# MLP first layer as a 2x2 block product with seven block products, its weight factors kept in DRAM

## The chip, the cores and the metric

The kernel runs on one core of one Trainium2 chip. The time is in device microseconds (us) for one execution. The engines are TensorE (PE in the profile, with PEld for its weight loads), VectorE (DVE), ScalarE (ACT), GpSimd (POOL) and SyncE (SP), which issues the transfers (DMA). All arithmetic is in float32.

## The reference

An attention block with normalised queries and keys feeds a two-layer MLP.

```python
batch, n_heads, seq, head_dim = (8, 12, 448, 64)
q_n, k_n = (rmsnorm(q, g_q), rmsnorm(k, g_k))
attn = softmax(q_n @ k_n.T / sqrt(head_dim))        # per batch and head
x = (attn @ v), heads side by side                  # 3584 tokens x 768
h = x @ w_in                                        # 768 x 2048
out = (h - tanh(h)) @ w_out                         # 2048 x 768
```

The weights arrive as float64, and the kernel rounds them to float32 itself.

## The kernel before

**Two streams on one TensorE.** The work is in 8 batches of 448 tokens. Attention goes by steps `s`, 48 of them: batch `b` and a pair of heads `hp`, six steps (`NP`) for each batch. A step normalises (`norm`, `norm_q`), transposes (`turn`), makes the scores and their exponentials in two halves (`scores`), multiplies with v (`values`), sums the exponentials (`totals`), and divides (`divide`: a reciprocal of 448 columns and a product on VectorE), which leaves one tile `xT` of 128 features x 448 tokens. The MLP of batch `b` runs beside the attention of batch `b+1`: `slot(s)` writes the attention step and, at four places in it, calls `run(gap)`, which takes matmuls from the stream `mlp()` until `gap` ns of it are written. The stream is `hidden(b)`, the first layer, and then `project(b)`, the second. The first six attention steps have no MLP beside them (`first_slot`), and the MLP of batch 7 has no attention beside it (`run(1e9)` at the end).

**The order is the program's.** The instructions stand on each engine as the Python code writes them (a manual schedule); each engine works through its own list and waits on semaphores, SP's list of transfers included.

**First layer.** `hidden(b)` makes, for each of 16 blocks `f` of 128 hidden features, six matmuls (`c`, blocks of 128 input features) of 128 x 128 weights by 448 columns into one bank of PSUM; then ScalarE makes tanh and VectorE subtracts it (`gT`). A float32 matmul stands in the trace as two weight loads and two passes. The weights `w_in_sb` lie in SBUF for the whole run.

**Second layer.** `project(b)` makes for each of three (four in odd batches) blocks of 128 tokens and each half `n` of 384 output columns 16 matmuls of 384 columns. `EARLY`, `weight(to)` and `weight_load(n)` are the weights' way in: 64 pieces of 384 KB in float64 words (32 of `w_in`, 32 of `w_out`) are loaded and rounded by `round_weight_a` (ScalarE, two instructions, L71 and L72), `round_weight_b` (VectorE, three: L78, L79, L82) and `round_weight_c` (GpSimd, L90). Twenty pieces are done by the end of the first six steps, 28 more inside `hidden(0)`, 16 inside `project(0)`.

## Time and profile before

| | |
|---|---|
| time, median of 3 runs | 1652.33 us (1651.37 to 1653.82) |
| the profiled execution's own time | 1652.88 us |
| its span, first to last instruction | 1651.0 us |
| PE busy | 1595.7 us, 97% |
| PE matmuls of line L338 (first layer) | 1536 passes, 598.9 us |
| PE matmuls of line L378 (second layer) | 1536 and 256 passes, 516.6 and 85.4 us |
| DVE, ACT, POOL busy | 633.1, 402.6, 320.5 us |
| bytes moved by DMA | 70.22 MB, mean 43 GB/s |

A row of the timeline has the start, the time taken and the engine, line, operation and tiles of one instruction or of several alike (xN). A row of the windows has a stretch, its length, and the busy time of each engine in it with the number of instructions. In the table of groups the two numbers behind the bar are the busy time of all and the mean ns of one. A row of the waits has the total, how often, and the longest.

### The profile page before, as it was taken

Reading aid. Unit: us, or ns where it says so; the run is one execution under the profiler, and the core shown is the slowest. Engines: PE = TensorE matmul, PEld = TensorE weight load, DVE = VectorE, ACT = ScalarE, POOL = GpSimd, SP = SyncE. Lnnn points to the kernel's source line nnn. Section 1 sums busy time; section 2 is a strip of 40 time slices with the busy share of each in tenths; the row PEclk is TensorE's granted clock in tenths of the full one; section 3 lists DMA queues with packets and bytes.
Section 4 is the critical chain, followed back from the end, with each engine's and each line's share of the span. In section 5 each row is a group of like instructions: output and inputs, shape, how many; then the busy total and the mean of one; then the engine's idle time right before and its main releaser. Section 6 shows DMA issues by size and latency. Waiting matters only on the chain.

```text
span 1651.0 us, 14103 instructions
## 1 busy us (share of the span) xinstructions
PE 1595.7 (97%) x5512; PEld 793.5 (48%) x5512; DVE 633.1 (38%) x769; ACT 402.6 (24%) x765; POOL 320.5 (19%) x222
## 2 busy tenths in 40 slices
PE   3889998999999999999999999999999999999998
PEld 1334454544554445544455444554455544555554
DVE  5788877234323432243333334323432243221100
ACT  4454453222221222122212221112222122201100
POOL 4644444111111112111211112111211111000000
PEclk8999999999999999999999999999999999999999
DMA  9432243100111011001001100110001100000000
GB/s 244 120 104 75 67 141 110 45 17 17 29 46 32 17 25 35 31 22 33 23 27 34 41 17 17 32 48 17 17 27 48 31 17 23 11 15 5 1 19 21
DMA packets 93585, 70.22 MB, mean 43 GB/s; under 512 B 48453, under 2 KB 89413, under 8 KB 93509
## 3 DMA queue, kind: packets, MB, share of 16 engines
q1 hardware_dynamic: 93184, 69.23, 14.8%
q8 instruction: 45, 0.74, 0.2%
q14 instruction: 32, 0.25, 0.0%
q10 hardware_dynamic: 324, 0.00, 0.0%
HBM read 58.20 MB, written 11.01 MB: 42 GB/s over the span
## 4 chain that ended last, share of the span: by engine, by line
PE 91%; DVE 4%; DMA 2%; issue 1%; POOL 1%; ACT 1%; SPq 0%; ACTq 0%; POOLq 0%; DVEq 0%
PE mm L338 35%; PE mm L378 33%; PE sc L271 9%; PE av L298 9%; PE dn L310 3%; DMA w_raw<-in_moe_w_out_dram 1%; PE sc L249 1%; PE sc L254 1%; DMA k_nat<-in_k_dram 1%; DVE rd L319 1%; POOL sq L224 1%; DVE rr L225 0%; DVE w_in L79 0%; DVE w_out L79 0%; DVE w_in L82 0%
## 5 line engine op out<-in xcount | busy, mean ns | idle before, releaser
L338 PE MATMUL mm<-xT,w_in 128*128 128x448 f32 x1536 | 598.9, 544 | 3.2 <-DVE gT L345 1.7
L378 PE MATMUL mm<-w_out,gT 128*128 128x384 f32 x1536 | 516.6, 492 | 3.7 <-POOL w_out L90 3.7
L338 PEld LDWEIGHTS mm<-xT,w_in 128*128 128x128 f32 x1536 | 284.9, 190 | 300.3 <-issue 283.2
L378 PEld LDWEIGHTS mm<-w_out,gT 128*128 128x128 f32 x1536 | 286.9, 191 | 228.0 <-issue 36.0
L276 ACT ACTIVATE p<-sc,rr 112x448 f32<-112x448 f32 x384 | 211.9, 637 | 405.4 <-PE sc L271 322.8
L319 DVE RECIPROCAL rd<-dn 128x448 f32<-128x448 f32 x48 | 141.9, 2956 | 202.0 <-PE dn L310 201.6
L345 DVE TENSOR_TENSOR gT<-mm,th 128x448 f32<-128x448 f32 x128 | 79.7, 623 | 333.6 <-ACT th L344 333.6
L344 ACT ACTIVATE th<-mm 128x448 f32<-128x448 f32 x128 | 69.6, 544 | 465.6 <-PE mm L338 458.6
L271 PE MATMUL sc<-qT,kT 64*112 64x448 f32 x768 | 173.7, 567 | 3.2 <-ACT qT L258 3.2
L224 POOL TENSOR_TENSOR sq<-k_nat 112x512 f32<-112x512 f32 x48 | 51.5, 1073 | 629.2 <-DMA k_nat<-in_k_dram 629.2
L298 PE MATMUL av<-p,v_nat 112*64 112x448 f32 x768 | 156.4, 549 | 6.8 <-issue 6.8
L228 POOL TENSOR_TENSOR rr<-rr,neg_half 112x16 f32<-112x16 f32 x48 | 139.3, 2902 | 51.0 <-DVE rr L227 47.8
L290 DVE TENSOR_TENSOR sum<-sum,p 112x896 f32<-112x896 f32 x84 | 94.3, 1123 | 93.3 <-ACT p L276 88.0
L271 PEld LDWEIGHTS sc<-qT,kT 64*112 64x112 f32 x768 | 63.2, 174 | 101.0 <-issue 86.4
L225 DVE TENSOR_REDUCE rr<-sq 112x8 f32<-112x512 f32 x96 | 65.6, 683 | 109.8 <-POOL sq L224 109.8
L298 PEld LDWEIGHTS av<-p,v_nat 112*64 112x64 f32 x768 | 52.3, 138 | 100.3 <-issue 100.3
L224 POOL TENSOR_TENSOR sq<-q_nat 112x512 f32<-112x512 f32 x48 | 49.9, 1039 | 240.7 <-DVE rr L225 240.7
L378 PE MATMUL mm<-w_out,g_rest 128*128 128x384 f32 x256 | 85.4, 489 | 0.0
L235 DVE TENSOR_TENSOR n<-q_nat,rr 112x512 f32<-112x512 f32 x48 | 42.0, 875 | 95.0 <-PE sc L254 72.8
L388 DVE COPY o_sb<-mm 128x384 f32<-128x384 f32 x28 | 15.5, 555 | 158.2 <-PE mm L378 157.9
L378 PEld LDWEIGHTS mm<-w_out,g_rest 128*128 128x128 f32 x256 | 47.9, 190 | 35.6 <-issue 4.1
L386 ACT COPY o_sb<-mm 128x384 f32<-128x384 f32 x28 | 13.4, 478 | 189.3 <-PE mm L378 125.1
(49 smaller groups left out, 598.6 us busy)
## 6 DMA issues: line engine op xcount, KB each, us to landing
w_out<-in_moe_w_in_dram SPq DMA_DIRECT2D x32, 384.0 KB, 7.6
k_nat<-in_k_dram SPq DMA_DIRECT2D x96, 112.0 KB, 3.1
q_nat<-in_q_dram SPq DMA_DIRECT2D x48, 224.0 KB, 3.5
v_nat<-in_v_dram SPq DMA_DIRECT2D x48, 224.0 KB, 3.4
w_raw<-in_moe_w_out_dram SPq DMA_DIRECT2D x24, 384.0 KB, 3.1
out_dram<-o_sb SPq DMA_DIRECT2D x48, 192.0 KB, 1.9
w_out<-in_moe_w_out_dram SPq DMA_DIRECT2D x8, 384.0 KB, 3.3
out_dram<-o_sb SPq DMA_DIRECT2D x16, 96.0 KB, 2.2
```

The costliest lines, as they stand in the source:

```text
L224: nc.gpsimd.tensor_tensor(out=sq, in0=rows, in1=rows, op=ALU.mult)
L225: nc.vector.reduce_sum(rr[:, i], sq, axis=AX.X)
L228: nc.gpsimd.tensor_tensor(out=rr2, in0=rr2, in1=neg_half, op=ALU.pow)
L271: nc.tensor.matmul(sc[:CP, :S], lhsT=kT[r, c * CP : (c + 1) * CP], rhs=qT[r, :], start=True, stop=True)
L276: nc.scalar.activation(p[:, h, i, :], tiles[h][:CP, :S], AF.Exp, scale=rr[:, 0, 2 * c + h : 2 * c + h + 1])
L290: nc.vector.tensor_tensor(out=t, in0=t, in1=part, op=ALU.add)
L298: nc.tensor.matmul(av[h * D : (h + 1) * D, :S], lhsT=v_nat[:, h, c, :], rhs=p[:, h, c % 2, :], start=(c == 0), stop=(c == NCH - 1),)
L319: nc.vector.reciprocal(rd, dn[:, :S])
L338: nc.tensor.matmul(hps[:, :S], lhsT=w_in_sb[f][:, c, :], rhs=xT[b, c], start=(c == 0), stop=(c == CD - 1))
L344: nc.scalar.activation(th, hps[:, :S], AF.Tanh, bias=0.0, scale=1.0)
L345: nc.vector.tensor_tensor(out=g[:, f, :], in0=hps[:, :S], in1=th, op=ALU.subtract)
L378: nc.tensor.matmul(ops[:, :HALF], lhsT=lhs[:, f, :], rhs=w_out_sb[f][:, d], start=(f == 0), stop=(f == CF - 1),)
```

## The change

Each batch's product of 448 tokens x 768 by 768 x 2048 is taken as 2 x 2 blocks (tokens in halves of 224, input features in halves of 384, hidden features in halves of 1024) and made with seven block products in place of eight (a scheme of the Strassen kind with shared sums). `hidden(b)` works in four sets `j` (two blocks of 128 from each half of the hidden features), each of seven products in the order `ORDER`; a product is six matmuls of 128 x 128 weights by 224 columns into one bank, and adds up in PSUM with another one where the scheme lets it (`first` false). Sums between banks are made on VectorE and GpSimd, copies out of a bank on ScalarE.

The seven weight factors of each set are made once (`combine_weights`, eight rounded pieces to seven factors), written to DRAM (`keep_weights`, seven stores of 384 KB), and read back for each product of each batch into a ring of eight tiles (`ring_load`), seven products ahead. `w_in_sb` is gone. The factors of the tokens' side are made in `divide` from the pair of `xT` tiles three steps apart (VectorE for batch 0, GpSimd after). Raw pieces are prefetched up to 6 ahead (14 before). In `first_slot` and `slot` the sums of the exponentials and the reciprocal now come ahead of the product with v. The four gaps of a slot are sized by batch; for batch 0 the whole first layer goes into two slots and the second layer into four. The core of the diff:

```diff
+    HS = S // 2
+    HC = CD // 2
+    SETS = CF // 4
+    ORDER = (1, 6, 5, 2, 7, 3, 4)
...
+    ring = pool("ring", bufs=8)
+    scratch = pool("scratch", bufs=1, space=bass.MemoryType.DRAM)
...
-    ps_v = pool("ps_v", bufs=1, space=PSUM)
-    ps_m = pool("ps_m", bufs=2, space=PSUM)
+    ps_m = pool("ps_m", bufs=1, space=PSUM)
+
+    def mm_bank(tag):
+        return ps_m.tile([P, 512], F32, name=tag, bufs=2 if tag == "mb" else 1)
...
-    w_in_sb = [weights.tile([P, CD, P], F32, name=f"w_in{f}") for f in range(CF)]
+    w_in_dram = {
+        (j, p): scratch.tile([P, 2 * HALF], F32, name=f"w_in{j}_{p}") for j in range(SETS) for p in range(1, 8)
+    }
...
+    stage = gp.tile([P, CF, S], F32, name="gT").bitcast(I32).rearrange("p f s -> p (f s)")
+    NSTAGE = CF * S // DM
...
+    def built(j, p):
+
+        return w_out_sb[CF // 2 * (j % 2) + p].rearrange("p (f n) -> p f n", f=2)
...
         if n < 2 * CF:
+            j, f, blk = n // 8, n % 8 // 4, n % 4
+            p, low, i = ((1, 0, 0), (0, 1, 0), (4, 1, 1), (2, 0, 1))[blk]
+            return 2 * j + f + low * CF // 2, i, built(j, p)[:, f]
...
+        if n < EARLY:
+            raw = stage[:, n % NSTAGE * DM : (n % NSTAGE + 1) * DM].rearrange("p (f w) -> p f w", w=2)
...
-        if n < CF or 0 <= n - 2 * CF - CF // 2 < 3:
-            return True
-        return n - (CF if n < 2 * CF else CF // 2 if n < 2 * CF + CF // 2 else 3) < done[2]
+        if n < EARLY:
+            return n - NSTAGE < done[2]
+        return n - 4 < max(done[2], EARLY)
...
+            finish_weights(n - 1 if n < EARLY else n)
+            while done[0] < min(n + 6, 4 * CF) and place_free(done[0]):
                 weight_load(done[0])
                 done[0] += 1
+            if kept[1] < kept[0] and n >= 8 * kept[0] + 3:
+                keep_weights()
...
+            if done[2] % 8 == 0 and done[2] <= 2 * CF:
+                combine_weights(done[2] // 8 - 1)
+
+    def combine_weights(j):
+        a = [built(j, p) for p in range(8)]
+        nc.vector.tensor_tensor(out=a[5], in0=a[0], in1=a[4], op=ALU.add)
+        nc.gpsimd.tensor_tensor(out=a[7], in0=a[1], in1=a[0], op=ALU.subtract)
+        nc.vector.tensor_tensor(out=a[6], in0=a[5], in1=a[1], op=ALU.subtract)
+        nc.vector.tensor_tensor(out=a[3], in0=a[2], in1=a[6], op=ALU.subtract)
+        kept[0] = j + 1
+
+    def keep_weights():
+        j = kept[1]
+        for p in ORDER:
+            nc.sync.dma_start(out=w_in_dram[j, p], in_=built(j, p).rearrange("p f n -> p (f n)"))
+        kept[1] = j + 1
...
+    ring_steps = [(b, j, p) for b in range(B) for j in range(SETS) for p in ORDER]
+    ring_tiles = {}
+
+    def ring_load(to):
+
+        for n in range(len(ring_tiles), min(to, len(ring_steps))):
+            b, j, p = ring_steps[n]
+            assert kept[1] > j
+            t = ring_tiles[ring_steps[n]] = ring.tile([P, 2, HC, P], F32, name="w_f")
+            nc.sync.dma_start(out=t.rearrange("p f c n -> p (f c n)"), in_=w_in_dram[j, p])
...
-    def totals(s):
-        dn = ps_v.tile([P, 512], F32, name="dn")
...
-        return dn
-
-    def divide(s, av, dn):
-        b, hp = steps[s]
         rd = sp.tile([P, S], F32, name="rd")
         nc.vector.reciprocal(rd, dn[:, :S])
+        return rd
+
+    def divide(s, av, rd):
+        b, hp = steps[s]
         x = xT[b, hp] = xp.tile([P, S], F32, name="xT")
...
+        if hp < HC:
+            return
+        c = hp - HC
...
+        eng = nc.vector if b == 0 else nc.gpsimd
+        x11, x12, x21, x22 = (xT[b, r][:, n : n + HS] for r in (c, hp) for n in (0, HS))
+        t1, t2, t4 = (tt[b][:, i, c] for i in range(3))
+        eng.tensor_tensor(out=t1, in0=x12, in1=x11, op=ALU.subtract)
+        eng.tensor_tensor(out=t2, in0=x22, in1=t1, op=ALU.subtract)
+        eng.tensor_tensor(out=x12, in0=x22, in1=x12, op=ALU.subtract)
+        eng.tensor_tensor(out=t4, in0=x21, in1=t2, op=ALU.subtract)
...
+        def product(j, p, bank, first):
             if b == 0:
-                weight(EARLY + (3 * CF - EARLY) * (f + 1) // CF)
-            for c in range(CD):
-                nc.tensor.matmul(
-                    hps[:, :S], lhsT=w_in_sb[f][:, c, :], rhs=xT[b, c], start=(c == 0), stop=(c == CD - 1)
-                )
+                weight(EARLY + k + 1)
+            ring_load(k + 7)
+            w = ring_tiles[b, j, p]
+            ring_tiles[b, j, p] = None
+            for f in range(2):
+                for c in range(HC):
+                    nc.tensor.matmul(
+                        bank[:, f * HS : (f + 1) * HS], lhsT=w[:, f, c, :], rhs=moving[p](c),
+                        start=(first and f == 0 and c == 0), stop=(f == 1 and c == HC - 1),
+                        skip_group_check=not first,
+                    )
+                    if f == 0 or c < HC - 1:
+                        yield 4 * HS / ENGINE_NS
+            now = later[:]
+            later.clear()
+            for fn in now:
+                fn()
...
+        pending = None
+        for j in range(SETS):
+            ma = mm_bank("ma")
+            yield from product(j, 1, ma, True)
+            s1 = part("s1", 2)
+            nc.scalar.copy(out=s1, in_=view(ma))
+            yield took
+            if pending:
+                yield from pending()
+            mb = mm_bank("mb")
+            yield from product(j, 6, mb, True)
+            s2 = part("s2", 2)
+            nc.vector.tensor_tensor(out=s2, in0=view(mb), in1=s1, op=ALU.add)
+            yield took
+            mc = mm_bank("mc")
+            yield from product(j, 5, mc, True)
+            s5 = part("s5")
+            nc.scalar.copy(out=s5, in_=view(mc))
+            yield took
+            yield from product(j, 2, ma, False)
+            shrink(j, 0, low, view(ma), nc.vector)
+            yield took
+            yield from product(j, 7, mb, False)
+            u3 = part("u3")
+            nc.vector.tensor_tensor(out=u3, in0=view(mb), in1=s1, op=ALU.add)
+            nc.gpsimd.tensor_tensor(out=u3, in0=u3, in1=s5, op=ALU.add)
+            later.append(lambda j=j, u3=u3: shrink(j, 1, high, u3, nc.gpsimd))
+            yield took
+            yield from product(j, 3, mc, False)
+            nc.vector.tensor_tensor(out=s2, in0=view(mc), in1=s2, op=ALU.add)
+            later.append(lambda j=j, s2=s2: shrink(j, 0, high, s2, nc.gpsimd))
+            yield took
+
+            def pending(j=j, mb=mb, s1=s1):
+                yield from product(j, 4, mb, False)
+                nc.vector.tensor_tensor(out=s1, in0=view(mb), in1=s1, op=ALU.add)
+                later.append(lambda: shrink(j, 1, low, s1, nc.gpsimd))
+                yield took
+
+        yield from pending()
+        for fn in later:
+            fn()
...
+        ring_load(SETS * 7 * (b + 1) + 7)
...
-    per_slot = (4 * S / ENGINE_NS * CF * CD + 4 * HALF / ENGINE_NS * CF * 7) / NP
+    H_NS = 4 * HS / ENGINE_NS * 7 * 6 * SETS
+    O_NS = 4 * HALF / ENGINE_NS * 2 * CF
+
+    def gap_ns(s):
+
+        b = s // NP - 1
+        if b == 0:
+            return H_NS / 8 if s % NP < 2 else O_NS * FULL / (4 * (NP - 2))
+        return (H_NS + O_NS * (FULL + b % 2)) / (4 * NP)
...
-            av = values(s)
+            rd = totals(s, mm_bank("mc"))
...
+            av = values(s, mm_bank("ma"))
...
-        divide(s, values(s), totals(s))
+        rd = totals(s, sc_bank())
+        divide(s, values(s, sc_bank()), rd)
```

On TensorE, at the start of `hidden(1)`, before, from the last rows of `project(0)` on (`mm` the MLP's bank, `sc` the scores' bank; a row's last number counts matmuls, each of them two passes):

```order
L378 MATMUL mm<-w_out_164,gT 128x384
L338 MATMUL mm<-xT,w_in_133 128x448 x6
L249 MATMUL sc<-ident,k_nat 128x112 x4
L254 MATMUL sc<-ident,n 128x112 x4
L338 MATMUL mm<-xT,w_in_134 128x448 x6
L338 MATMUL mm<-xT,w_in_135 128x448 x2
L271 MATMUL sc<-qT,kT 112x448 x4
```

The same place after (`w_f` a tile of the ring, `tt` a sum of blocks of `xT`, `ma`, `mb`, `mc` the MLP's banks; L353 is `values`, L365 `totals`, now ahead of it):

```order
L427 MATMUL ma<-xT,w_f 128x224 x6
L427 MATMUL mb<-tt,w_f 128x224 x6
L427 MATMUL mc<-tt,w_f 128x224 x5
L365 MATMUL sc<-sum,ones 64x448 x2
L353 MATMUL sc<-p,v_nat 64x448 x8
L427 MATMUL mc<-tt,w_f 128x224
L427 MATMUL ma<-xT,w_f 128x224 x6
```

The six matmuls of 448 columns for one weight block have become six of 224 columns for one product, each product with weights from the ring, and a bank is asked for again two or more products later.

On SP, in the second slot of `hidden(0)`, before: raw pieces of the second layer's weights between the loads of q, k and v.

```order
L180 DMA w_out_157<-in_moe_w_out_dram 128x768
L144 DMA k_nat<-in_k_dram 112x4x64 x2
L147 DMA q_nat<-in_q_dram 112x2x256
L180 DMA w_out_158<-in_moe_w_out_dram 128x768
L180 DMA w_out_159<-in_moe_w_out_dram 128x768
```

The same place after (L206 a raw piece, L257 a store of `keep_weights`, L269 a load of the ring):

```order
L206 DMA w_raw_1375<-in_moe_w_out_dram 128x768
L257 DMA w_in3_1_175<-w_out9_147 128x768
L257 DMA w_in3_6_180<-w_out14_152 128x768
L257 DMA w_in3_5_179<-w_out13_151 128x768
L257 DMA w_in3_2_176<-w_out10_148 128x768
L257 DMA w_in3_7_181<-w_out15_153 128x768
L257 DMA w_in3_3_177<-w_out11_149 128x768
L257 DMA w_in3_4_178<-w_out12_150 128x768
L269 DMA w_f_1384<-w_in3_1_175 128x768
L206 DMA w_raw_1404<-in_moe_w_out_dram 128x768
L269 DMA w_f_1406<-w_in3_6_180 128x768
```

Seven stores now stand in the list ahead of the load that reads the first of them back, and every raw piece has a ring load beside it.

On VectorE, in the first slot of `hidden(0)`, after (L78, L79, L82 round one piece; L248, L250, L251 are `combine_weights`; L467 and L472 add banks). Before, such a stretch holds only pieces and L345 (`gT`), one L345 for about two pieces.

```order
L78 TENSOR_SCALAR w_out_140<-w_out_140 128x384
L79 TENSOR_SCALAR w_out_140<-w_out_140 128x384
L82 SCALAR_TENSOR_TENSOR w_out_140<-w_raw,w_out_140 128x384
L248 TENSOR_TENSOR w_out_143<-w_out_138,w_out_142 128x768
L250 TENSOR_TENSOR w_out_144<-w_out_143,w_out_139 128x768
L251 TENSOR_TENSOR w_out_141<-w_out_140,w_out_144 128x768
L467 TENSOR_TENSOR u_1104<-mb,s_1000 128x448
L78 TENSOR_SCALAR w_out_147<-w_out_147 128x384
L79 TENSOR_SCALAR w_out_147<-w_out_147 128x384
L82 SCALAR_TENSOR_TENSOR w_out_147<-w_raw,w_out_147 128x384
L472 TENSOR_TENSOR s_1019<-mc,s_1019 128x448
```

The additions that free a bank for TensorE now stand behind the three instructions of a piece and, once in seven products, behind the three of `combine_weights`.

82 lines of the change are left out of this document (44 added, 38 removed).

## The prediction

> **What bounds the kernel now.** I read the page first: the busy shares and the chain that ended last.
>
> ```profile
> PE 1595.7 (97%) x5512; PEld 793.5 (48%) x5512; DVE 633.1 (38%) x769; ACT 402.6 (24%) x765; POOL 320.5 (19%) x222
> PE 91%; DVE 4%; DMA 2%; issue 1%; POOL 1%; ACT 1%; SPq 0%; ACTq 0%; POOLq 0%; DVEq 0%
> ```
>
> TensorE carries the span, so only its work and its waits count. Next come the windows, cut where the first six steps' start-up ends (46), where the MLP of batch 0 begins (118.5), where its first layer ends (217), where batch 1's MLP begins (316.24), and one later batch.
>
> ```profile
> 0.00:46.00 46.00, 13.76 (x48) 6.68 (x49) 26.04 (x42) 18.33 (x36) 25.30 (x23) 0.85 0.89 231
> 46.00:118.50 72.50, 65.66 (x329) 26.64 (x328) 54.40 (x68) 38.95 (x78) 41.76 (x29) 0.98 0.44 120
> 118.50:217.00 98.50, 95.28 (x313) 44.55 (x313) 86.55 (x127) 47.27 (x97) 43.64 (x36) 1.00 0.24 71
> 217.00:316.24 99.24, 92.19 (x321) 46.64 (x320) 59.82 (x86) 34.18 (x68) 38.41 (x30) 0.97 0.34 102
> 316.24:511.00 194.76, 194.76 (x677) 96.78 (x675) 66.19 (x74) 41.21 (x77) 30.90 (x19) 1.00 0.10 29
> ```
>
> The columns after the length are PE, PEld, DVE, ACT, POOL, clock, DMA share, GB/s. From 316 on TensorE never stops, and every other engine is under 35% busy. While weights are rounded (118.5 to 217) VectorE is at 88%. So there are two regimes: seven batches bound by TensorE alone, and batch 0, where the weights' way in is nearly as long as the matmuls.
>
> The price of a pass is cleanest at the end, where the MLP of batch 7 runs alone (timeline of TensorE).
>
> ```profile
> 1490.12 72.32 PE L338 MATMUL mm<-xT,w_in 128*128 128x448 f32 x192
> 1562.28 62.08 PE L378 MATMUL mm<-w_out,gT 128*128 128x384 f32 x192
> 1624.20 20.80 PE L378 MATMUL mm<-w_out,g_rest 128*128 128x384 f32 x64
> ```
>
> From start to start: 72.16 us for 192 passes of 448 columns, 375.8 ns each; 61.92 us for 192 of 384, 322.5 ns. That is 0.833 ns a column and 2.5 ns fixed.
>
> **The change, term by term.**
>
> *First layer, the gain.* Before, 96 matmuls a batch, 192 passes of 448. After, 28 products of six matmuls, 336 passes of 224. By the line above a pass of 224 takes 189.1 ns, 63.5 us a batch in place of 72.2: 8.6 us less.
>
> No row shows a float32 pass that short with 128 rows and 128 columns of weights, so I bound it. These rows show small passes and the weight loads (PEld):
>
> ```profile
> 320.75 0.55 PE L249 MATMUL sc<-ident,k_nat 112*128 112x112 f32 x4
> 321.13 0.55 PE L254 MATMUL sc<-ident,n 112*128 112x112 f32 x4
> 321.52 6.19 PE L338 MATMUL mm<-xT,w_in 128*128 128x448 f32 x16
> 353.47 0.55 PE L249 MATMUL sc<-ident,k_nat 112*128 112x112 f32 x4
> 354.15 0.30 PEld L338 LDWEIGHTS mm<-xT,w_in 128*128 128x128 f32 x2
> 1490.49 0.19 PEld L338 LDWEIGHTS mm<-xT,w_in 128*128 128x128 f32 x1 [0.19 <-issue]
> 1490.87 0.19 PEld L338 LDWEIGHTS mm<-xT,w_in 128*128 128x128 f32 x1 [0.19 <-issue]
> ```
>
> Four transposes of 112 columns, each with its own load, take 0.38 us from start to start, 96 ns each: on the same line, so a load behind each short pass cost nothing there. A load of the first layer takes 190 ns by itself, but two of them end within 0.30 us, so a second one begins about 110 ns after the first. Loads start with the pass before (1490.49 is one pass after 1490.12) and are over half-way through it. If only the 110 ns must fit beside a pass of 187 ns, it does. If the whole 190 ns must, a pass takes 190 to 192, and the gain falls by 0.3 to 1.0 us a batch. The good end is the proportional one, 187.9 ns: 0.4 us more. I take 189.1, the fit of two rows of the same form. Not hidden at all is a rival below.
>
> The Trainium skill speaks against this: its page "TensorE: Matmul & The Clock Gate", Part 3, under "The mechanism", says that a weight load overlaps matmuls in flight only when it goes to another row group. All loads here take all 128 rows, so by that rule they would overlap nothing. The trace disagrees at 448 columns, where 375.8 ns a pass leaves no room for a load.
>
> *What goes with it in batches 1 to 7.* For each set ScalarE has six instructions in place of four (544 ns by the group below), VectorE five in place of four (623), GpSimd four new ones of 448 columns (about 940 by its 512 columns in 1073). GpSimd also gets twelve of 224 columns a batch, about 0.5 us each.
>
> ```profile
> L345 DVE TENSOR_TENSOR gT<-mm,th 128x448 f32<-128x448 f32 x128 | 79.7, 623 | 333.6 <-ACT th L344 333.6
> L344 ACT ACTIVATE th<-mm 128x448 f32<-128x448 f32 x128 | 69.6, 544 | 465.6 <-PE mm L338 458.6
> L224 POOL TENSOR_TENSOR sq<-k_nat 112x512 f32<-112x512 f32 x48 | 51.5, 1073 | 629.2 <-DMA k_nat<-in_k_dram 629.2
> ```
>
> That is 4.4 us more on ScalarE, 2.5 on VectorE and 21 on GpSimd for a batch of some 186 us, where they had 41, 66 and 31. All stay under 70 us, and a bank is asked for again at least two products (4.5 us) later, so TensorE covers it; without that cover each late sum would show in full. I allow 0.5 us a batch for short waits at the products' seams, 0 to 2 for the range.
>
> The ring brings 28 x 384 KB = 11.0 MB a batch. The rows that price a transfer:
>
> ```profile
> q1 hardware_dynamic: 93184, 69.23, 14.8%
> w_raw<-in_moe_w_out_dram SPq DMA_DIRECT2D x24, 384.0 KB, 3.1
> 15.00:25.00 10.00, 4.83 (x16) 2.14 (x16) 8.15 (x13) 5.99 (x13) 7.05 (x6) 1.00 1.10 332
> ```
>
> 69.23 MB in 14.8% of 1651 us is 283 GB/s while it moves; the fullest stretch had 332. So 11.0 MB take 33 to 39 us of a first layer that lasts about 90 us beside attention and 63.5 alone, asked for seven products ahead (16 us, against 3.1 to land). Hidden. On SP each ring load waits for the product eight before it; the q, k and v loads queued behind stand in program order near the same matmuls and have two slots of lead.
>
> *Batch 0.* Between the two transposes at 320.75 and 353.47 lies one slot, with four runs of 16 passes: 32.72 - 64 x 0.3758 = 8.7 us of attention on TensorE a slot. Before, batch 0 took 197.7 us (118.5 to 316.24) for 72.2 + 61.9 + 6 x 8.7 = 186.3 us of matmuls; the other 11 are waits:
>
> ```profile
> PE mm L378 <- POOL w_out L90: 3.7, 2, 2.7
> PE sc L271 <- ACT qT L258: 2.6, 1, 2.6
> PE mm L338 <- DVE gT L345: 1.7, 1, 1.7
> PE mm L338 <- DVE xT L321: 1.5, 1, 1.5
> PE av L298 <- issue: 6.8, 5, 1.4
> ```
>
> (the last is of the first six steps). After, the first layer and its 28 pieces share two slots, 63.5 + 2 x 8.7 = 81 us on TensorE. VectorE in these slots, by the groups of the window 118.5 to 217:
>
> ```profile
> L79 DVE TENSOR_SCALAR w_in<-w_in 128x384 int32<-128x384 int32 x14 | 9.3, 665 | 0.5
> L82 DVE SCALAR_TENSOR_TENSOR w_in<-w_out,w_in 128x384 int32<-128x384 int32 x14 | 9.3, 661 | 0.5
> L78 DVE TENSOR_SCALAR w_in<-w_in 128x384 f32<-128x384 f32 x14 | 6.1, 433 | 0.0
> L288 DVE TENSOR_TENSOR sum<-p 112x896 f32<-112x896 f32 x3 | 3.8, 1271 | 0.0
> ```
>
> A piece is 1.76 us, 28 are 49. Twenty additions at 623 are 12.5. Six of `combine_weights`, 768 columns against 896 in 1271, are 6.5. Attention has (66.19 - 16 x 0.623 - about 2 for outputs) / 6 = 9 us a slot, 18. Together 86 us, now more than TensorE, and before VectorE lost 12 of 98.5 us to waits of its own. The transfers in the same stretch: 28 raw pieces, 28 ring loads, 14 stores (sets 2 and 3) and up to 7 of set 1, 77 x 0.393 MB, and 1.4 MB of q, k, v: 31.7 MB, 95 us at 332 GB/s and 112 at 283, of which the last 10 us of the first steps take a part. So 87 (VectorE alone, no waits) to 112; I take 100, since two resources at their limit seldom fit together. The second layer's four slots are 61.9 + 4 x 8.7 = 96.7 plus 6 for waits (16 pieces in two of them; 10 before with 44 pieces in six slots): 102.7. Batch 0 becomes 202.7, 5.0 more.
>
> The skill's page "DMA: Bandwidth & Descriptors", in its table at the top, has about 358 GB/s as the limit of HBM for a core. By that figure those bytes would take an estimated 89 us, and the term would be some 5 us less.
>
> *The first 118.5 us.* The chain there:
>
> ```profile
> 11.55 12.88 SPq L175 DMA_DIRECT2D w_out<-in_moe_w_in_dram x12
> 24.60 0.93 SPq L144
> 25.58 8.51 DMA k_nat<-in_k_dram
> 34.24 1.05 POOL sq L224
> ```
>
> and on GpSimd:
>
> ```profile
> 24.56 3.42 POOL L90 TENSOR_TENSOR w_in<-w_in,w_out 128x384 int32<-128x384 int32 x3
> ```
>
> SP issued 12 raw pieces before the third step's k, which landed at 34.1. With six pieces ahead rather than 14 it issues four there, so k lands some 10 us earlier; GpSimd is free for it from 28, so 6 us come off. The 6.8 us of "av <- issue" go too if VectorE lets them: `totals` now stands first, so its reciprocal runs beside scores and `values`. But VectorE gets six combining additions (6.5 us) and twelve small ones (about 4): 54.4 + 10.5 = 65 of 72.5 us, so I count 2 of the 6.8. What is late next is the first ring tile: seven stores of set 1 (2.75 MB, 8.3 to 9.7 us) are queued ahead of it, about one step before the first product; 4 us. Net -4, between -12 and +6.
>
> **The sum**, against the profiled execution, 1652.88 us, which is its span of 1651.0 and 1.9 around it, and 0.5 above the median:
>
> - batches 1 to 7: -7 x 8.6 = -60.3
> - seams: +3.5
> - batch 0: +5.0
> - start: -4
>
> 1652.9 - 55.8 = 1597.
>
> **Rivals.**
>
> 1. *Batch 0 becomes a chain through DRAM.* The factors of a set can be read only after pieces, combination and stores; the ring cannot run ahead of that. If nothing covers it, each of sets 1 to 3 costs 9.7 us of stores and 3.1 to land, 38 in all, on top of the sum in place of my 4 at the start: about 1631. For it: VectorE at 88% already and the seven stores ahead of the first load. Against: eight products lie between combining a set and needing it.
> 2. *The ring is late in every batch.* If SP's waits let only one load at a time be under way, a product alone lasts 3.1 us and not 2.27; 21 products of batch 7 then cost 17 us more, and beside attention (a product each 3.1 us or so) nothing unless q, k and v loads collide, some 3 us a batch: 1614 to 1635. Against: eight buffers.
> 3. *Slower: weight loads are not hidden behind short passes.* Place: every first-layer pass. If a pass takes 187 + 110 = 297 ns, a batch costs 99.8 us, 27.6 more than before, eight times 221: about 1870. It decides from 72.16 / 336 = 215 ns a pass on. For it: the load's 190 ns is as long as the pass, and PEld would be near 100% in the first layer. Against: the transposes at 96 ns. It is what the skill's rule on row groups would do here.
>
> **Chances and range.** My forecast 0.70, rival 1 0.12, rival 2 0.06, rival 3 0.06; 0.03 for a start and batch 0 that both gain (around 1578), 0.03 for mishaps that eat the gain within 0.2% or beyond. A change under 0.2% (3 us) is about what a measurement of this kernel can't tell from none. Faster: 0.70 + 0.12 + 0.06 + 0.03, less 0.02 for rivals 1 and 2 together, 0.89; of the 0.11 left, 0.02 is the same and 0.09 slower. The range: below, passes at 187.9 (-3), seams at 0 (-3.5), start at -12 (-8) and batch 0 at 95 (-5) would give 1577; above, rivals 1 and 2 reach 1635, of which I leave the last bit out: 1577 to 1630.
>
> **What would show it.** Right: first-layer passes 189 ns apart in the last batch, whose hidden part takes 63.5 us; batch periods about 8 us shorter from the second MLP batch on, with TensorE without a pause; batch 0 about 200 us with VectorE above 85%. Wrong: waits of the first-layer matmuls on ring transfers after batch 0, passes at 200 ns or more, or batch 0 well over 215 us with TensorE waiting for DMA or at a lower clock after long pauses.

## The result and the profile after

| | before | after |
|---|---|---|
| median, runs on the same chip | 1651.85 us (1648.51 to 1653.82, 4 runs) | 1610.93 us (1609.97 to 1612.2, 4 runs) |
| ratio, 95% interval | | 0.9755 (0.9737 to 0.9772) |
| span of the profiled execution | 1651.0 us | 1608.6 us |
| first layer of batch 0 begins | 118.53 us | 119.59 us |
| batch 0, first layer and second | 101.9 + 95.8 us | 108.0 + 109.2 us |
| batches 1 to 6, first product to first product of batch 7 | 1173.88 us | 1119.71 us |
| first layer of batch 7, alone | 72.16 us | 63.56 us |

The changed kernel is faster by 41 us; 1597 was forecast, so it is 14 us slower than that. The engines' busy times on the page after:

```profile
PE 1542.8 (96%) x6664; PEld 1018.9 (63%) x6664; DVE 697.1 (43%) x825; ACT 436.4 (27%) x829; POOL 549.8 (34%) x438
PE 82%; DVE 11%; issue 2%; DMA 2%; POOL 1%; ACT 1%; SPq 0%; ACTq 0%; DVEq 0%; POOLq 0%
```

TensorE's share of the chain that ended last fell from 91% to 82%, and VectorE's rose from 4% to 11%: a stretch now ends on VectorE that did not before. The end of the run shows the gain by itself (timeline of TensorE, batch 7 alone).

```profile
1456.44 2.43 PE L427 MATMUL ma<-xT,w_f 128*128 128x224 f32 x12
1458.71 2.43 PE L427 MATMUL mb<-tt,w_f 128*128 128x224 f32 x12
...
1517.73 2.43 PE L427 MATMUL mb<-tt,w_f 128*128 128x224 f32 x12
1520.00 62.08 PE L515 MATMUL mb<-w_out,gT 128*128 128x384 f32 x192
```

28 products follow each other every 2.27 us, 189.2 ns for each of 336 passes. No product waits for weights, sums or a bank, though weight loads (PEld) are busy for all of the 63.56 us. From 336.73 to 1520.00 TensorE's list of waits is empty. The windows of batch 0 (columns PE, PEld, DVE, ACT, POOL, clock, DMA share, GB/s), with the last stretch of the first six steps ahead of it:

```profile
108.40:119.59 11.19, 0.09 (x1) 0.00 (x0) 10.88 (x12) 2.88 (x6) 5.59 (x3) 0.69 1.00 352
119.59:227.57 107.98, 91.52 (x425) 76.55 (x425) 95.79 (x133) 45.32 (x94) 64.85 (x50) 0.91 0.73 244
227.57:336.73 109.16, 104.35 (x370) 51.55 (x369) 74.51 (x93) 39.42 (x78) 57.27 (x47) 0.95 0.37 106
```

Before, TensorE was busy for 95.28 of 98.5 us in that place at a clock of 1.00. Now it stands still for 11 us ahead of the first product while VectorE works without a break, waits 16.5 us more in the first layer, and runs at a granted clock of 0.91 and 0.95. What it waited for from 115 to 340 us:

```profile
PE ma L427 <- DVE xT L376: 11.1, 1, 11.1
PE ma L427 <- DVE gT L416: 5.8, 2, 5.4
PE mb L427 <- DVE u L467: 5.3, 2, 2.7
PE sc L327 <- DVE rd L370: 4.3, 2, 2.3
PE mc L427 <- DMA w_f<-w_in: 2.8, 1, 2.8
PE mb L427 <- DVE s L455: 2.5, 1, 2.5
```

All but one are VectorE's; the ring has one wait in the whole run, 2.8 us. VectorE's dearest groups in the first layer of batch 0 (119.59 to 227.57):

```profile
L79 DVE TENSOR_SCALAR w_out<-w_out 128x384 int32<-128x384 int32 x29 | 25.0, 862 | 1.0
L78 DVE TENSOR_SCALAR w_out<-w_out 128x384 f32<-128x384 f32 x29 | 16.3, 564 | 2.3 <-ACT w_out L71 2.3
L82 DVE SCALAR_TENSOR_TENSOR w_out<-w_raw,w_out 128x384 int32<-128x384 int32 x26 | 14.5, 558 | 0.9
...
L251 DVE TENSOR_TENSOR w_out<-w_out,w_out 128x768 f32<-128x768 f32 x2 | 4.8, 2377 | 0.2
L250 DVE TENSOR_TENSOR w_out<-w_out,w_out 128x768 f32<-128x768 f32 x2 | 3.3, 1653 | 0.1
```

L79 had a mean of 665 ns before and has 862 now, L78 433 and 564, with the same shapes; L82 fell from 661 to 558.

### The profile page after: what moved, and what is told of

Read it like the earlier page. It is cut to its first block, busy times and chain, and to the rows that moved or that the text cites. A ratio compares the mean times of both kernels' runs of the same rounds, so it can differ in the third digit from the quotient of the medians.

```text
span 1608.6 us, 17479 instructions
## 1 busy us (share of the span) xinstructions
PE 1542.8 (96%) x6664; PEld 1018.9 (63%) x6664; DVE 697.1 (43%) x825; ACT 436.4 (27%) x829; POOL 549.8 (34%) x438
## 4 chain that ended last, share of the span: by engine, by line
PE 82%; DVE 11%; issue 2%; DMA 2%; POOL 1%; ACT 1%; SPq 0%; ACTq 0%; DVEq 0%; POOLq 0%
PE mb L515 34%; PE mb L427 12%; PE ma L427 8%; PE mc L427 8%; PE sc L327 8%; PE sc L353 7%; DVE w_out L79 3%; PE sc L365 2%; DVE rd L370 2%; DVE w_out L78 1%; POOL sq L280 1%; DVE w_out L82 1%; DVE rr L281 1%; PE sc L303 1%; PE sc L307 1%
## 5 line engine op out<-in xcount | busy, mean ns | idle before, releaser
L515 PE MATMUL mb<-w_out,gT 128*128 128x384 f32 x1536 | 518.2, 492 | 0.0
L515 PEld LDWEIGHTS mb<-w_out,gT 128*128 128x128 f32 x1536 | 287.4, 191 | 221.5 <-issue 37.8
L427 PE MATMUL ma<-xT,w_f 128*128 128x224 f32 x768 | 164.7, 362 | 16.9 <-DVE xT L376 11.1
L427 PEld LDWEIGHTS ma<-xT,w_f 128*128 128x128 f32 x768 | 146.4, 194 | 33.0 <-issue 13.7
L427 PE MATMUL mb<-tt,w_f 128*128 128x224 f32 x768 | 156.7, 357 | 5.3 <-DVE u L467 5.3
L370 DVE RECIPROCAL rd<-sc 128x448 f32<-128x448 f32 x42 | 124.0, 2953 | 86.7 <-PE sc L365 86.7
L427 PEld LDWEIGHTS mb<-tt,w_f 128*128 128x128 f32 x768 | 144.9, 192 | 16.0 <-issue 8.6
L353 PE MATMUL sc<-p,v_nat 112*64 112x448 f32 x672 | 133.4, 539 | 0.0
L353 PEld LDWEIGHTS sc<-p,v_nat 112*64 112x64 f32 x672 | 48.3, 137 | 78.0 <-issue 76.8
L427 PE MATMUL mb<-xT,w_f 128*128 128x224 f32 x384 | 83.0, 360 | 2.5 <-DVE s L455 2.5
L515 PE MATMUL mb<-w_out,g_rest 128*128 128x384 f32 x256 | 85.4, 489 | 0.0
```

What stands on the lines that cost most here:

```text
L353: nc.tensor.matmul(av[h * D : (h + 1) * D, :S], lhsT=v_nat[:, h, c, :], rhs=p[:, h, c % 2, :], start=(c == 0), stop=(c == NCH - 1),)
L370: nc.vector.reciprocal(rd, dn[:, :S])
L427: nc.tensor.matmul(bank[:, f * HS : (f + 1) * HS], lhsT=w[:, f, c, :], rhs=moving[p](c), start=(first and f == 0 and c == 0), stop=(f == 1 ...
L515: nc.tensor.matmul(ops[:, :HALF], lhsT=lhs[:, f, :], rhs=w_out_sb[f][:, d], start=(f == 0), stop=(f == CF - 1),)
```

## The experiments

The theory after the result: the steady batches gain what a shorter first layer gives, and batch 0 gives a part of it back because VectorE's list (rounding, combining, sums) sets its end. The rivals: that the way through DRAM does it (stores, the read back, SP's list), and that the order of the attention steps, and not the products, makes a part of the difference. The places of the MLP in the runs, in us (e4 and e11, which lengthen every batch, stand further down); the second layer of batch 0 ends where batch 1 begins:

| run | time | batch 0 begins | first layer | second layer | batch 1 begins |
|---|---|---|---|---|---|
| before | 1651.85 | 118.5 | 101.9 | 95.8 | 316.2 |
| after | 1610.93 | 119.6 | 108.0 | 109.2 | 336.7 |
| e1 no rounding on VectorE | 1583.65 | 120.2 | 92.1 | 96.7 | 309.1 |
| e2 ring from q, no stores | 1607.85 | 119.4 | 108.2 | 106.1 | 333.7 |
| e3 three slots | 1623.79 | 119.8 | 130.8 | 97.7 | 348.4 |
| e5 additions to GpSimd | 1621.31 | 126.9 | 113.6 | 105.9 | 346.4 |
| e6 sums by TensorE | 1601.9 | 116.0 | 104.2 | 107.6 | 327.8 |
| e7 order undone | 1619.4 | 130.3 | 109.9 | 105.9 | 346.1 |
| e8 before, order and prefetch | 1638.25 | 106.5 | 100.9 | 93.2 | 300.6 |
| e9 banks exchanged | 1611.63 | 116.2 | 115.1 | 106.9 | 338.2 |
| e10 e6 and e9 together | 1601.45 | 115.9 | 106.5 | 105.9 | 328.3 |

In all of these but before and e8 the batches from 1 on are those of after to within 0.1 us (198.1 and 177.5 us in turn, the last one beside attention 170.4). The runs e1 to e4, e5 to e8 and e9 to e11 were made on different chips, where the kernel before had medians of 1652.76, 1651.15 and 1650.22 us, so a difference of 1 or 2 us between two of these groups means nothing.

### VectorE or the way through DRAM (e1, e2)

In `weight`, e1 leaves VectorE's rounding of 44 pieces out:

```diff
-                round_weight_b(nc, raws[n - 1], weight_piece(n - 1)[2])
+                if n - 1 < EARLY:
+                    round_weight_b(nc, raws[n - 1], weight_piece(n - 1)[2])
...
-            round_weight_b(nc, raws[4 * CF - 1], weight_piece(4 * CF - 1)[2])
```

> The three VectorE instructions of a piece (L78, L79, L82) are left out for the 44 pieces that are rounded beside batch 0's MLP, so the weights of these pieces are not the reference's; everything else, transfers included, stays. VectorE theory (batch 0 took 217 us because VectorE is full, 57 us of pieces in the first layer alone): batch 0's MLP takes about 190 us, the time is 1580 to 1588. Transfer theory (the raw pieces, stores and ring loads, or the way through DRAM, set the pace): no more than 8 us come off, 1603 to 1611.

1583.65 us (1583.35 to 1584.88), ratio to before 0.9584 (0.9568 to 0.96), 27.3 us below the changed kernel. Its windows of batch 0:

```profile
120.23:212.36 92.13, 84.60 (x424) 72.23 (x424) 47.71 (x54) 45.24 (x95) 63.66 (x52) 0.96 0.83 285
212.36:309.10 96.74, 96.74 (x370) 49.06 (x368) 43.07 (x39) 38.53 (x77) 53.97 (x45) 1.00 0.40 119
```

VectorE is busy for half the first layer. The transfers are the same and now move 285 GB/s, so the DMA rate of 244 was not what held batch 0. Nor was GpSimd's own work, 63.66 us here and 64.85 in the changed kernel. What is left of TensorE's waits in this first layer is 4.8 us for one ring tile and 2.7 for VectorE; the 11.1 us ahead of the first product stay. The second layer takes 96.74 us without a pause at full clock, what its matmuls and four slots of attention come to (96.7).

In e2 the ring reads a part of `q` of the same size, and nothing is stored:

```diff
-        for p in ORDER:
-            nc.sync.dma_start(out=w_in_dram[j, p], in_=built(j, p).rearrange("p f n -> p (f n)"))
...
-            nc.sync.dma_start(out=t.rearrange("p f c n -> p (f c n)"), in_=w_in_dram[j, p])
+            src = bass.AP(tensor=q.tensor, offset=(7 * j + p - 1) * P * 2 * HALF, ap=[[2 * HALF, P], [1, 2 * HALF]])
+            nc.sync.dma_start(out=t.rearrange("p f c n -> p (f c n)"), in_=src)
```

> The 28 stores of weight factors are left out, and the ring reads blocks of q of the same size in place of the factors, so it never waits for a store (the products are not the reference's). VectorE theory: batch 0 still takes 210 us or more, 2.8 us of ring wait go, the time is 1603 to 1611. Transfer theory: 15 to 25 us come off, 1586 to 1596. In both, batches 1 to 7 stay at 186 to 187 us.

1607.85 us (1607.38 to 1608.05), 0.9732 (0.9716 to 0.9748): 3 us below the changed kernel, and batch 1 begins 3.0 us earlier in the trace. With no stores and no dependence on them, the waits from 108 to 230 us are (L423 is L427 of the changed kernel, four lines up):

```profile
PE ma L423 <- DVE xT L372: 11.1, 1, 11.1
PE ma L423 <- DVE gT L412: 8.1, 2, 7.7
PE mb L423 <- DVE u L463: 5.5, 2, 2.9
PE mb L423 <- DVE s L451: 3.1, 2, 2.5
```

VectorE's waits stay and take the place of the one ring wait. The way through DRAM costs 3 us here; the theory that it holds batch 0 falls.

### Work moved off VectorE or spread out (e3, e5, e6)

e3 gives the first layer of batch 0 three slots in place of two:

```diff
-            return H_NS / 8 if s % NP < 2 else O_NS * FULL / (4 * (NP - 2))
+            return H_NS / 12 if s % NP < 3 else O_NS * FULL / (4 * (NP - 3))
```

> Batch 0's first layer is spread over three slots of attention in place of two, its second layer over three in place of four; nothing else. VectorE theory: 28 pieces share three slots, VectorE's 108 us of work there stand beside 63.5 + 26 = 90 us of TensorE and not 91 beside 81, so the waits in the first layer shrink, but 16 pieces then stand in less time: 5 to 12 us come off, 1599 to 1606. If the number of slots doesn't matter because VectorE's total over six slots does: 1609 to 1612.

1623.79 us (1622.11 to 1626.06), 0.9832 (0.9814 to 0.985), 13 us slower than the changed kernel and outside both expectations, with the first layer 22.8 us longer and the second 11.5 shorter. VectorE was busy for 102.55 of the 130.84 us; its own waits there:

```profile
DVE rr L281 <- POOL sq L280: 17.7, 6, 7.3
DVE w_out L78 <- ACT w_out L71: 6.8, 2, 3.4
```

The third slot's attention joined VectorE's list, and brought a wait for GpSimd's squares of k, in one of which GpSimd itself waited 5.1 us for k's load. That this load was late because it stands in SP's list behind raw pieces and ring loads fits the order of that list; no run took them apart. More room for TensorE did not help where the engine that sets the pace got more to do and new waits.

e5 gives the three additions of `combine_weights` and the tokens' factors of batch 0 to GpSimd:

```diff
-        nc.vector.tensor_tensor(out=a[5], in0=a[0], in1=a[4], op=ALU.add)
+        nc.gpsimd.tensor_tensor(out=a[5], in0=a[0], in1=a[4], op=ALU.add)
...
-        eng = nc.vector if b == 0 else nc.gpsimd
+        eng = nc.gpsimd
```

(and the other two alike)

> All four instructions of combine_weights and batch 0's sums of xT blocks go to GpSimd; the result is the reference's. If only VectorE's own length counts: it loses 10 us in the first layer of batch 0 (two sets of 5.0) and 6 to 9 in the first six steps, so 8 to 15 us come off, 1596 to 1603. If what counts is VectorE and GpSimd slowing each other (L79 took 0.36 us alone and 1.06 beside GpSimd) and the wait of the stores for the combination: three more instructions of about 2.4 us a set on GpSimd give it back, 1609 to 1620.

1621.31 us (1619.98 to 1624.04), 0.9824 (0.9799 to 0.9848): 10.4 us slower than the changed kernel, as the second theory had it (1609 to 1620). The instruction of VectorE ahead of the late start, the window of the first layer, and three groups of VectorE in it:

```profile
114.08 0.69 DVE L281 TENSOR_REDUCE rr<-sq 112x8 f32<-112x512 f32 x1 [9.71 <-POOL sq L280]
...
126.90:240.50 113.60, 93.97 (x425) 78.30 (x425) 100.21 (x125) 45.36 (x95) 78.33 (x60) 0.88 0.69 231
L79 DVE TENSOR_SCALAR w_out<-w_out 128x384 int32<-128x384 int32 x29 | 29.0, 999 | 1.0
L82 DVE SCALAR_TENSOR_TENSOR w_out<-w_raw,w_out 128x384 int32<-128x384 int32 x27 | 21.2, 785 | 0.9
L78 DVE TENSOR_SCALAR w_out<-w_out 128x384 f32<-128x384 f32 x29 | 19.0, 654 | 2.9 <-ACT w_out L71 2.9
```

The start is 7.3 us later. VectorE stands still there for 9.7 us, waiting for GpSimd's squares of k, which stand in GpSimd's list behind the four instructions of `combine_weights` (105.81 to 113.05 us). In the first layer VectorE has 8 instructions fewer than in the changed kernel and is busy for 4.4 us more, since all three of a piece's instructions got dearer (L79 862 to 999, L82 558 to 785, L78 564 to 654) with GpSimd busy for 78 us and not 65. So work given to GpSimd cost VectorE twice, once by the place of other work in GpSimd's list and once in its own durations; the start is the larger part of what was lost.

e6 leaves VectorE's sums of the exponentials out for three more steps, which TensorE then adds up in PSUM:

```diff
-        if s < NP:
+        if s < NP + 3:
             sums[s] = []
```

> For the three attention steps beside batch 0's first layer and its end the sums of the exponentials are made by TensorE (16 passes in totals in place of 4, about 2.3 us more a step) and not by three additions on VectorE (4.7 us in the trace). VectorE theory: 3 x 4.7 = 14 us of VectorE go and 7 us of TensorE come where it has pauses; the 11.1 us wait ahead of the first product shrinks by about 4 as well: 10 to 16 us come off, 1595 to 1601. If VectorE isn't what counts: 7 us slower, 1618.

1601.9 us (1600.71 to 1602.07), 0.9698 (0.9676 to 0.9721), 9.0 us below the changed kernel and, with e10, the best version found; the VectorE theory had 1595 to 1601. Batch 0 begins 3.6 us earlier and takes 5.4 less; in its first layer VectorE has 89.15 us in place of 95.79 and TensorE 92.73 in place of 91.52. TensorE's longest wait inside this first layer is now for a ring tile:

```profile
PE mc L427 <- DMA w_f<-w_in: 7.3, 1, 7.3
```

### Order (e7, e8)

e7 takes the changed kernel and puts the product with v ahead of the sums again:

```diff
-            rd = totals(s, mm_bank("mc"))
+            av = values(s, mm_bank("ma"))
...
-        rd = totals(s, sc_bank())
-        divide(s, values(s, sc_bank()), rd)
+        av = values(s, sc_bank())
+        divide(s, av, totals(s, sc_bank()))
```

> One part undone: values stands ahead of totals again, in the first six steps and after; the seven products stay. Expected: the wait of 1.3 us on the divide comes back in five of the first steps (slots of 12.2 in place of 10.9), but batch 0 was bound by VectorE behind it, so 3 to 7 us slower, 1614 to 1618; batches 1 to 6 lose nothing or up to 0.4 us each, the part of their gain (9.0 us a batch measured, 8.6 from the passes) that the passes don't explain.

1619.4 us (1617.81 to 1620.07), 0.9803 (0.978 to 0.9826). The start is 10.7 us later, more than the 3 to 7 expected, batch 0 1.3 shorter, the rest the same.

e8 takes the kernel before and gives it that order and the shorter prefetch alone:

```diff
-            while done[0] < min(n + CF - 2, 4 * CF) and place_free(done[0]):
+            while done[0] < min(n + 6, 4 * CF) and place_free(done[0]):
...
-            av = values(s)
+            rd = totals(s)
```

(with the reciprocal in `totals`)

> The other part alone: the kernel before, with totals and its reciprocal ahead of values and raw pieces prefetched 6 ahead, and no block product. If the gain of the change is the passes' alone: 0 to 7 us under before in the first 118 us (the third k earlier, no wait on the divide) and nothing later, 1645 to 1652. If the order brings part of the steady gain: 3 us more.

1638.25 us (1637.14 to 1639.19), 0.9923 (0.9899 to 0.9946): 13 us below before, where 0 to 7 were expected. Its first product follows the scores without a pause (timeline of TensorE):

```profile
104.64 1.94 PE L271 MATMUL sc<-qT,kT 64*112 64x448 f32 x8
106.50 4.03 PE L338 MATMUL mm<-xT,w_in 128*128 128x448 f32 x10
```

The start gains 12.0 us and batch 0 3.6; batches 1 to 6 are those of before (209.3 and 183.5 us in turn). So 13 us of the 41 could be had without any product; what the order and what the prefetch brings of them was not taken apart. Measured against e8, the products' kernel gets to batch 1 36.1 us later (336.7 against 300.6), and wins 62.8 from there on.

### The wait ahead of the first product (e9, e10)

The first product wants bank `ma`, in which the last of the first six steps left its product with v, and the division that frees it stands last in VectorE's list. e9 exchanges the banks, so that only the reciprocal is waited for; e10 does it on top of e6.

```diff
-            rd = totals(s, mm_bank("mc"))
+            rd = totals(s, mm_bank("ma"))
...
-            av = values(s, mm_bank("ma"))
+            av = values(s, mm_bank("mc"))
```

> Only the banks are exchanged in the first six steps: the sums of the exponentials go to bank ma and the product with v to mc, so that the first product, which wants ma, waits for the reciprocal (ended at 112.1 us after the change) and no longer for the division (119.53). If the 11.1 us in front of the first product are no more than a bank that is late, and cost what they last, the first product starts near 112.2, all else moves up by as much, and the time is about 1603.5 us. If VectorE's list sets the end of batch 0 (it was busy for 95.8 of 108.0 us of the first layer), the start moves as much but the second product waits for its tokens' factors (ended at 120.8) and the first layer takes longer by most of what was won: 1608 to 1611 us, and the 109 us of the second layer stay.

> The exchange of banks together with TensorE summing the exponentials in three more steps (that alone gave 1601.9 us). If VectorE's list sets batch 0: the first product starts near 112.5 (reciprocal), the second at about 117.3 when its factors are there and not at 120.6, and of these 3.3 us no more than 2 stay: 1599.5 to 1602. If the late bank costs what it lasts: 1594 to 1598. Batches 1 to 7 as before at 198.1 and 177.5 us in both.

e9 took 1611.63 us (1611.03 to 1612.9), 0.9764 (0.9748 to 0.9781), no less than the changed kernel; e10 1601.45 (1600.97 to 1602.43), 0.9701 (0.9685 to 0.9718), no less than e6. Rows of e9: the first product, and the windows of batch 0.

```profile
116.21 4.82 PE L427 MATMUL ma<-xT,w_f 128*128 128x224 f32 x12 [6.68 <-DVE sum L344]
116.21:231.31 115.10, 94.17 (x424) 78.14 (x424) 103.05 (x140) 45.83 (x95) 67.71 (x53) 0.89 0.74 251
231.31:338.18 106.87, 102.02 (x371) 50.23 (x369) 71.56 (x89) 39.30 (x77) 55.22 (x45) 0.98 0.34 98
```

The start came forward by 3.4 us, not the 7.4 expected. The row puts the wait down to a sum of VectorE, which the product doesn't read. The reciprocal had ended at 113.14, and the first ring tile landed at 116.08, 0.14 us before the product; in e10, where the row names the tile, it landed 0.14 us before the product as well. So the ring tile is the likely cause: in the changed kernel it landed at 115.24, hidden behind the bank, which came at 119.55. The first layer then took 7.1 more and the second 2.3 less; that the first layer ended 3.7 us later than in the changed kernel is not explained. The 11.1 us stand in the list of waits, and taking a third of them away was worth nothing: VectorE's list ended no sooner. In e10 the ring's waits are the longest:

```profile
PE mc L427 <- DMA w_f<-w_in: 7.7, 1, 7.7
PE ma L427 <- DMA w_f<-w_in: 7.5, 1, 7.5
```

The second is that of the first product; the first, near 165 us, is the tile that is late by 2.8 us in the changed kernel, 4.8 in e1 and 7.3 in e6. With VectorE relieved, tiles of the ring are what is late in batch 0. So e2's 3 us is the price of the way through DRAM beside a full VectorE; what it is beside a relieved one was not tried.

### Weight loads and the ring (e4, e11)

e4 splits every first-layer matmul into two of 112 columns with the same weights:

```diff
+                    for u in range(2):
...
-                        bank[:, f * HS : (f + 1) * HS], lhsT=w[:, f, c, :], rhs=moving[p](c),
+                            bank[:, f * HS + u * CP : f * HS + (u + 1) * CP], lhsT=w[:, f, c, :],
+                            rhs=moving[p](c)[:, u * CP : (u + 1) * CP],
```

> Each first-layer matmul of 224 columns is made as two of 112 with the same weights loaded again: 672 passes a batch. If a pass costs 0.833 ns a column and 2.5 ns whatever its length, 96 ns: batch 7's first layer alone takes 64.5 us, the time about 1618. If the 110 ns between two loads set the pace: 74 us, about 1690. If the whole 190 ns of a load does (the second rival of the forecast, moved to where it must show): 128 us, about 2120.

One run, 1690.39 us. Batch 7 alone:

```profile
1524.66 2.83 PE L428 MATMUL ma<-xT,w_f 128*128 128x112 f32 x24
1527.33 2.84 PE L428 MATMUL mb<-tt,w_f 128*128 128x112 f32 x24
1530.01 2.84 PE L428 MATMUL mc<-tt,w_f 128*128 128x112 f32 x24
```

2.68 us for 24 passes, 111.7 ns each, where 0.833 ns a column and 2.5 fixed would be 95.8. It is the pace that the 110 ns between two loads had led to expect; at 224 columns the loads did not set it.

e11 gives the ring two tiles in place of eight:

```diff
-    ring = pool("ring", bufs=8)
+    ring = pool("ring", bufs=2)
...
-            ring_load(k + 7)
+            ring_load(k + 2)
...
-        ring_load(SETS * 7 * (b + 1) + 7)
+        ring_load(SETS * 7 * (b + 1) + 1)
```

> The ring has two tiles in place of eight, so that one load is under way while one product runs. If what hides the factors' way back is the eight tiles (a load takes 3.3 us from issue to landing, a product alone 2.27): in the last batch each of 28 products waits about 1 us, its first layer takes 88 to 95 us in place of 63.6, and batches 1 to 6 grow by 0 to 8 us each where loads of q, k, v or raw pieces stand ahead in the list: 1637 to 1680 us. If the latency is hidden by the product under way alone, the last first layer stays at 63.6 us and the time at 1611.

1901.36 us (1898.99 to 1903.73, 2 runs), 1.152 (1.1494 to 1.1545). The last first layer took 93.7 us (1719.57 to 1813.30), within what was expected, but the other stretches were far out: 202.4 us for the first layer of batch 0, and 27 to 30 us more in each later one beside attention (115.0 against 87.0 in batch 1). TensorE's waits over the span:

```profile
PE ma L427 <- DMA w_f<-w_in: 114.5, 31, 17.6
PE mc L427 <- DMA w_f<-w_in: 58.1, 26, 13.0
PE mb L427 <- DMA w_f<-w_in: 43.9, 44, 2.4
```

Attention does not hide a late tile: between two places of attention nearly three products stand one behind the other (12, 12 and 10 passes from 336.73 us on in the changed kernel), and those wait as the lone ones do: 27 to 30 us beside attention, 30.2 alone. The waits come to 216 us; the granted clock fell to 0.94 as well. Eight tiles are what makes the ring free after batch 0.

## Why the prediction was right, and where it was off

**The pass: right.** 189.1 ns forecast, 189.2 measured; 8.60 us less for the last first layer, as worked out. Rival 3 is dead at 224 columns, although its sign came: weight loads are busy for all of the last first layer. A full PEld alone did not mean that loads set the pace, and e4 shows where loads begin to decide: between 112 columns, where they set 111.7 ns, and 224. The 110 ns between two loads was the right reading of the rows, not the 190 ns of one. By the rule of the Trainium skill on row groups ("TensorE: Matmul & The Clock Gate", Part 3, "The mechanism") no load here would overlap; the trace disagrees at 448, 224 and even at 112 columns. The same section also lets a load into the background weight buffer go ahead of matmuls in flight, which the forecast left out and with which these numbers agree. The same page's formula under "LDWEIGHTS (loading the stationary operand)" gives 107 ns for 128 columns, near e4's 111.7.

**Batches 1 to 7: -60.3 and +3.5 for seams forecast, -62.8 measured** (1246.04 us from 316.24 to 1562.28 before, 1183.27 from 336.73 to 1520.00 after). The seams cost nothing. Of the 2.5 us beyond 60.3 the cause is where the cut lies: batch 1's first product stood ahead of the transposes of a slot before, and stands behind them and the next half of the scores now.

```profile
316.24 4.67 PE L338 MATMUL mm<-xT,w_in 128*128 128x448 f32 x12
320.75 0.55 PE L249 MATMUL sc<-ident,k_nat 112*128 112x112 f32 x4
321.13 0.55 PE L254 MATMUL sc<-ident,n 112*128 112x112 f32 x4
```

(before) and

```profile
330.29 0.55 PE L303 MATMUL sc<-ident,k_nat 112*128 112x112 f32 x4
330.68 0.55 PE L307 MATMUL sc<-ident,n 112*128 112x112 f32 x4
...
335.04 1.76 PE L327 MATMUL sc<-qT,kT 64*112 64x448 f32 x8
336.73 2.54 PE L427 MATMUL ma<-xT,w_f 128*128 128x224 f32 x12
```

(after). Starts differ by 0.38 + 0.38 + 1.69 = 2.5 us of attention that has gone over to batch 0. "6 x 8.7" in the 197.7 us before counted them once too often, so the waits there were nearer 14 us than 11.

**Batch 0: +5.0 forecast, +19.4 measured. This is the step that failed**, by its size; its mechanism (VectorE as the bound) was named. The first layer took 108.0 us where 100 was taken, the second 109.2 where 102.7 was. Two terms were short:

- VectorE's list: a piece at 1.76 us measured 1.98 in the first layer (the three means above: 862 + 564 + 558 ns), and six additions of `combine_weights` at 1.08 each measured 10.0 us, not 6.5. These two make 9.7 us, the difference between the 86 us added up for VectorE and its 95.79. The prices were means of a stretch in which GpSimd had 43.64 us to do; with 64.85 beside it they no longer hold. The same instruction 7 us apart, once with GpSimd idle and once with it at work:

```profile
139.91 0.36 DVE L79 TENSOR_SCALAR w_out<-w_out 128x384 int32<-128x384 int32 x1
146.72 1.17 DVE L79 TENSOR_SCALAR w_out<-w_out 128x384 int32<-128x384 int32 x1
```

```profile
141.00 1.60 POOL L90 TENSOR_TENSOR w_out<-w_out,w_raw 128x384 int32<-128x384 int32 x1 [2.78 <-issue]
142.56 2.52 POOL L249 TENSOR_TENSOR w_out<-w_out,w_out 128x768 f32<-128x768 f32 x1
146.50 1.18 POOL L468 TENSOR_TENSOR u<-u,s 128x448 f32<-128x448 f32 x1 [1.43 <-DVE u L467]
```

- The clock: the second layer's 96.7 us of matmuls were costed at full speed. They took 104.35 at a granted clock of 0.95, and 4.8 of waits beside them, fewer than the 6 allowed. In e1, without VectorE's waits, they took 96.74 at 1.00. By the mean clock some 5.5 of the 7.7 us too many (an estimate, 0.05 x 109.16) are the clock's; the rest is not explained. A wait was paid twice, once as idle time and again in the passes behind it.

The transfers, taken as a second limit at 95 to 112 us, were not one: they came to 26.3 MB in the first layer (244 GB/s for 107.98 us) and not 31.7, e1 moved the same bytes in 92 us, and e2 gained 3. The stretch from 108.40 to 119.59 moved 352 GB/s, and the one from 160 to 170 moved 374. The second is above the about 358 GB/s that the Trainium skill has as the limit for a core ("DMA: Bandwidth & Descriptors", the table at the top), so the trace does not bear that limit out here.

**The start: -4 forecast, +1.1 measured.** The earlier k and the order are worth -12 by e8, the lower end of the range. The changed kernel has that gain too: TensorE's waits ahead of the first product were 38.4 us before (23.1 on `n`, 8.5 on k, 6.8 in front of `values`) and, without the last one, are 26.9 after (18.7 and 8.2). All of the 6.8 went, not 2; then the first product's one wait of 11.1 us for VectorE's division took it back (119.6 against 106.5). The forecast had no such wait. The stores and the late ring tile, put at 4 us, were not what held the start: e2 without stores starts at 119.4, and the tile landed at 115.24. They show once the bank comes earlier (e9) or VectorE is relieved (e10).

Together the seven batches came out 6.0 us better than forecast, batch 0 14.4 and the start 5.1 worse. The time lay 14 us above the forecast; that it was no more is partly the luck of misses that went both ways.

**Rivals 1 and 2.** The sets' chain through DRAM (38 us) is refuted by e2, which gained 3. The ring is never late after batch 0; but the price put on one load at a time, 1614 to 1635, was far too low, as e11's 1901 shows. It rested on attention hiding the tile, which it does not.

## What to carry to other kernels

A change that shortens the steady part and loads the start-up has to be priced in two lists, with the busiest helper engine's list added up for the start-up: here 62.8 us were won in seven batches, and 36 given back ahead of them against a kernel with the same order and no products (e8). A duration taken from a row holds for the company it had there; here VectorE's prices rose when a change gave GpSimd more work. A long wait in the list of waits is no price: ask what the waiting engine would run into next (e9 took 3.4 us off one of 11.1 and the time did not move, e6 shortened the list behind it and won 9).

## What was not expected of the hardware

Some of VectorE's instructions whose operands all lie in SBUF get three times dearer and more while GpSimd works: L79 0.36 us alone and 1.17 beside it, and with GpSimd given still more (e5) the mean rose from 862 to 999 ns. In the first layer of batch 0 the 29 records of L79 fall into two kinds: 10 with GpSimd idle, 359 to 361 ns each, and 19 with an instruction of GpSimd beside them, 1046 to 1315. VectorE's two-input addition of 768 columns took 0.95 us, and 1.65 and 2.37 as GpSimd's own subtraction ran beside it. Those that read PSUM did not change (L467 615 ns, against 623 for the kind before). The Trainium skill's page "GPSIMD Engine Reference", Section 1 "Specifications", has the interfaces to SBUF as shared between the two; the trace agrees.

After a pause TensorE is slow for a while: the first product behind the 11.1 us took 4.20 us for its 12 passes, where 2.43 is usual; the granted clock was 0.50 from 113 to 119 us and until 122.99, 3.4 us into the product.

```profile
119.59 4.20 PE L427 MATMUL ma<-xT,w_f 128*128 128x224 f32 x12 [11.10 <-DVE xT L376]
```
